# A hand-written queue of 782 entries, put into another order, with 113 of its copies on other engines

## The chip, the core and the metric

The kernel runs on one core of a Trainium2 chip. The metric is the device time of one execution in microseconds (us); of several runs the median counts. The core's engines work at the same time, each through its own queue in order: TensorE (PE; PEld is its weight load), VectorE (DVE), ScalarE (ACT), GpSimd (POOL) and SyncE (SP), which here issues nearly all DMA transfers.

## The reference

Attention with a few global keys and a local window, then a feed-forward layer with three first matrices of which the largest product counts. There are 4 batches, 8 heads, 768 positions and 64 dimensions a head; 8 global keys and a window of 96.

```python
keep = is_global | is_local                    # pos_k < 8, or 0 <= pos_q - pos_k < 96
scores = scale * (q @ k.T) - slope[h] * dist   # dist is capped to 96 at the global keys
a = softmax(where(keep, scores, -1e9))
x = (a @ v) as 3072 tokens of 8 heads * 64
h = maximum(maximum(x @ w1, x @ w2), x @ w3)   # 512 -> 768
out = h @ w_out                                # 768 -> 512
```

## The kernel before, in words

The 3072 tokens are 24 tiles T of 128, six to a batch. A tile attends to itself and to the tile ahead of it. The 8 global keys and their values are copied into the place of keys that are out of the window, in each tile that serves as the one ahead (G for keys, V for values), so that two key tiles are enough; for a batch's first tile G saves the global keys instead. The feed-forward part takes the tiles in seven chunks of 4, 2, 2, 4, 4, 4 and 4.

The whole order is written out by hand in the string SCHEDULE (lines 24 to 87). Each entry is a call of one of the small functions below; the instructions of each engine stand in its queue in the order of the entries. Nothing else plans: an engine waits at the head of its queue until the inputs are there and the buffer or bank that it writes has been read.

An entry is a letter, its arguments, and after @ the slot of the buffer ring or the PSUM bank that it writes. Its last argument, `how`, names the engine of a copy or cast: 0 is ScalarE, 1 VectorE, 2 GpSimd. So `c1.9.2.1` casts k of tile pair 9, both halves of the heads, on VectorE.

- l, w, q: loads of q, k and v (first argument 0, 1, 2), of w1..w3, of w_out (SP). r, rv and staging are their rings. Pair 12 stands for the first four tiles' q and k.
- c, W, Q: casts of these to bf16 (L195, or L201 in two halves on GpSimd). v: the cast of v into the tile `va` (L254).
- x, y: transposes of q and k through TensorE (L270, L276) and the copies out of PSUM (L283, L287); X: the same by one DMA transpose (L292). Both fill `qkT`.
- b, S: the bias and the scores of tile T, half g of the heads (L335, L349); e: the exponential (L356); m: the product with the mask (L365, L367). B and K make the bias and the mask. D are dummy matmuls.
- G, V: the copies of global keys and values (L313, L315; L321 to L325).
- A: scores times values (L391, L394), n: division by the sum (L402, L403) into `xb`; t, u: transposes of that through TensorE (L418, L421); Z: by DMA (L424). Both fill `xT`.
- F c.f.j: the product of chunk c, block f of 128 hidden columns, with matrix j (L433); f: a copy for j = 0 (L447), the maximum for j = 1 (L449) and j = 2 (L452) into `ht`.
- O: the second product of one tile (L457), o: its copy (L471), s: its store (L477). E is the last chunk's end (L479 to L505), whose banks and staging slots are listed in LAST_BANKS and LAST_STAGES.

PSUM has eight banks: F, O, x and t take one, S, b and A two neighbouring ones.

Of the kernel before, what the change touches and what calls it, by code (L numbers as in the profile page):

```python
# [21 lines left out]


SCHEDULE = """
    l0.12.1@0 l1.12.1@1 D10.512@0 l1.12.3@2 l0.12.2@3 l0.12.3@4 R K7 K6 B1.1 K4 B2.1 K2 B3.0 K1 K5 B0.1 B6.1
    K0 c0.12.3.2@0 l1.12.2@5 c0.12.1.1 B4.1 B5.1 c1.12.1.1@1 K3 x12.0.1@0 y0.0.1.0@0 B7.1 l2.0.2@0 D3.256@1
    x12.1.1@1 b0.1@2 v1.0.2 l2.1.2@1 c1.12.3.1 v1.1.2 b1.0@4 y0.1.1.0 b1.1@6 S1.1.1 l0.2.2@6 c0.12.2.1
    y1.0.1.1@1 y1.1.1.0 x12.0.2@0 e1.1@0 c1.12.2.1 x12.0.3 y0.0.0.1 l1.2.2@0 y1.0.0.1 x12.1.3@1 x12.1.2
    y0.1.0.0 S0.1.1 e0.1@1 G0.1 b2.1@6 v2.0.2 v3.0.2 w1.0@0 S1.0.1 G1.0 e1.0@2 b2.0@2 w0.0@0 y1.1.0.1 S2.1.1
    w1.1@1 S0.0.0@0 e0.0@3 l2.2.2@2 S2.0.1 v0.0.1 e2.0@4 w0.1@1 v0.1.1 m0.0.1 e2.1@5 v2.1.2 b3.0@4 A1@0  # L30
    V1.1.1 V1.0.2 G2.1 v3.1.2 w0.2@2 A0@2 S3.0.1 e3.0@6 b3.1@6 n1@0 c0.2.2.2@2 S3.1.1 G3.0 A2@0 V2.0.2
    e3.1@7 V2.1.2 n0@1 t0@2 W0.0.2 c1.2.2.1 u0.0@0 x2.1.2@3 y2.1.2.0@2 w1.2@2 x2.0.2@2 A3@4 t1@6 u1.0 n2@2
    y2.0.2.1 t2@7 n3@3 l0.3.2@1 l1.3.2@2 S4.1.0@0 V3.1.2 e4.1@0 V3.0.2 S4.0.0@2 W1.1.2 u2.1 t3@6 G4.1 u3.0
    W2.0.1 S5.1.0@4 e5.1@2 S5.0.0@0 e5.0@1 m4.1.1 W1.0.1 e4.0@3 F0.5.0@7 F0.4.0@6 W2.1.0 F0.3.0@4 f0.3.0.0@0
    F0.2.0@5 f0.4.0.1@1 F0.1.0@6 v4.1.2 v4.0.2 l2.3.2@0 f0.1.0.0@2 q2@0 v5.1.0 F0.0.0@0 F0.5.1@1 F0.4.1@4
    F0.2.1@6 m4.0.1 f0.0.0.0@3 v5.0.0 f0.5.0.0@4 m5.1.1 A4@2 V4.1.0 F0.3.1@0 W0.1.2 f0.4.1.1 W0.2.0 m5.0.1
    f0.5.1.1 F0.0.1@1 F0.1.1@4 V4.0.1 W1.2.0 n4@1 t4@7 A5@2 W2.2.0 c1.3.2.2@0 f0.0.1.1 f0.1.1.1 F0.1.2@1
    n5@0 u4.1@1 f0.1.2.1@0 F0.0.2@4 q0@1 t5@7 u5.0 q1@2 f0.3.1.1 f0.0.2.1 F0.2.2@2 F0.3.2@3 f0.3.2.1
    c0.3.2.0 f0.2.0.0@2 f0.2.1.1 F1.2.0@4 F1.0.2@7 Q2.0 v7.1.2 F1.0.0@5 f1.0.0.1@3 v6.1.2 F1.0.1@3 f0.2.2.1
    f1.0.1.1 f1.2.0.1@0 Q0.2 f1.0.2.1@1 x3.1.2@6 y3.1.2.1@3 F0.4.2@5 f0.4.2.1 l1.4.2@3 v6.0.2 Q1.2 F1.1.0@0  # L40
    F1.2.2@1 l0.4.2@4 l1.6.2@5 F1.2.1@4 f1.2.1.1 F1.3.1@2 f1.2.2.1 F1.3.2@3 v7.0.2 F1.3.0@4 f1.3.0.0@2
    f1.3.1.1 f1.3.2.1 x3.0.2@1 F0.5.2@5 f0.5.2.1 F1.4.0@2 F1.1.1@3 f1.1.0.0@3 y3.0.2.0 S6.0.0@0 S6.1.0@4
# [17 lines left out]
    l2.9.2@2 l0.8.2@5 c0.8.2.2@0 v19.0.2 V13.0.0 f3.2.0.0@0 v14.0.2 F3.5.1@0 l2.8.2@1 F3.2.1@6 f3.2.1.1  # L60
    f3.2.2.1 F3.3.1@1 F3.5.2@3 v18.1.0 X14@3 v14.1.2 X15 f3.5.1.1 f3.3.1.1 F3.4.1@2 c1.8.2.0 S14.0.0@4
    S14.1.0@0 e14.0@6 G14.2 f3.4.1.1 F3.4.2@6 f3.5.2.1 F3.3.2@7 e14.1@7 f3.4.2.1 m14.0.1 m14.1.1 v19.1.2
    v15.0.2 S15.0.0@0 e15.0@0 S15.1.0@2 G15.1 e15.1@5 f3.3.2.1 O2.0@6 A14@0 V14.1.2 o2.0.1@6 n14@3 X18@0
    O2.1@7 v18.0.0 o2.1.0@7 m15.0.1 S18.0.0@0 S18.1.0@2 X19 Z13@1 V14.0.1 O3.3@6 m15.1.1 e18.0@3 e18.1@4
# [6 lines left out]
    G19.0 s0.1 V19.0.2 s2.1 f4.1.1.1 f4.1.2.1@0 V19.1.1 F4.0.0@4 F4.4.1@5 A17@2 c1.10.2.0 f4.0.0.1@3 n17@2
    F4.5.1@7 f4.5.1.1 F4.2.1@1 F4.3.2@4 f4.5.2.1 f4.4.1.1 F4.0.2@2 F4.3.1@3 F4.4.2@5 f4.2.1.1 v22.1.1
    f4.0.1.1 f4.3.1.1 f4.0.2.1 f4.3.2.1 F4.2.2@1 Z17 F5.1.1@0 F5.2.0@3 F5.5.0@2 s1.1 F5.3.0@4 F5.0.0@6
    f4.2.2.1 f5.3.0.0@4 f5.0.0.0@3 v21.1.2 F5.1.0@1 s0.0 l1.11.2@0 F5.3.1@4 c1.11.2.2 f5.2.0.1@0 f4.4.2.1
    v23.0.2 F5.0.1@3 v21.0.2 f5.1.0.1@2 f5.1.1.1 s2.0 X20@2 S20.0.0@0 v22.0.1 S20.1.0@6 f5.0.1.1 G20.2
    f5.5.0.0@1 e20.0@3 e20.1@4 F5.5.1@2 f5.5.1.1 F5.2.2@3 v20.1.2 f5.3.1.1 F5.2.1@5 m20.1.1 F5.4.0@2
    f5.2.1.1 m20.0.1 f5.2.2.1@1 F5.1.2@4 f5.1.2.1 X21 f5.4.0.0@0 s3.3 X23@3 s0.3 S21.1.0@0 S21.0.0@6 e21.0@2
    F5.0.2@3 X22 f5.0.2.1 v23.1.2 e21.1@6 s0.2 A20@4 F5.4.1@2 V20.0.1 m21.0.1 F5.4.2@3 G21.1 S22.1.0@0
# [533 lines left out]
```

## Time and profile before

| | |
|---|---|
| median of three runs | 175.69 us (175.66 to 176.38) |
| the profiled execution | 176.69 us, span 174.8 us |
| busy: PE, DVE, ACT, POOL | 165.9, 131.9, 95.4, 54.7 us |
| DMA | 37.36 MB, 214 GB/s on average |
| TensorE's granted clock | 0.996 over the span |

The span runs from the first to the last instruction of the program; the execution's own time has 1.9 us around it. Times in the rows are from the span's start. In a group's row stand, behind x and the count, the busy time in us, the mean of one in ns, then the engine's idle time ahead of the group and what ended most of it. A row of the timeline or of the chain gives start and length in us. A row of the windows gives the stretch, its length, then busy us and instructions of each engine, the granted clock of TensorE, the share of the DMA engines and GB/s. In the row of a wait stand the total, the number of times and the longest.

### The profile page before, as it was taken

Reading aid. Unit: us, or ns where it says so; the run is one execution under the profiler, and the core shown is the slowest. Engines: PE = TensorE matmul, PEld = TensorE weight load, DVE = VectorE, ACT = ScalarE, POOL = GpSimd, SP = SyncE. Lnnn points to the kernel's source line nnn. Section 1 sums busy time; section 2 is a strip of 40 time slices with the busy share of each in tenths; the row PEclk is TensorE's granted clock in tenths of the full one; section 3 lists DMA queues with packets and bytes.
Section 4 is the critical chain, followed back from the end, with each engine's and each line's share of the span. In section 5 each row is a group of like instructions: output and inputs, shape, how many; then the busy total and the mean of one; then the engine's idle time right before and its main releaser. Section 6 shows DMA issues by size and latency. Waiting matters only on the chain.

```text
span 174.8 us, 3865 instructions
## 1 busy us (share of the span) xinstructions
PE 165.9 (95%) x1485; PEld 93.6 (54%) x1507; DVE 131.9 (75%) x268; ACT 95.4 (55%) x147; POOL 54.7 (31%) x99
## 2 busy tenths in 40 slices
...
GB/s 149 352 292 327 402 360 385 270 371 311 229 303 179 139 183 266 267 290 284 165 135 112 114 145 306 305 210 260 231 213 20 0 120 137 121 286 4 0 119 185
DMA packets 66403, 37.36 MB, mean 214 GB/s; under 512 B 24144, under 2 KB 61392, under 8 KB 66384
## 3 DMA queue, kind: packets, MB, share of 16 engines
...
q8 instruction: 12, 0.20, 0.5%
...
## 4 chain that ended last, share of the span: by engine, by line
PE 76%; DVE 10%; DMA 6%; ACT 3%; issue 2%; SPq 0%; DVEq 0%
PE psum L433 44%; PE psum L457 17%; PE psum L349 6%; DMA xT<-xb 3%; DMA rawqk<-in_k_dram 3%; DVE P L365 3%; PE psum L391 3%; PE psum L394 2%; PE psum L276 2%; DVE ht L452 1%; DVE xb L403 1%; ACT P L356 1%; PE psum L270 1%; DVE qb L195 1%; PE psum L335 1%
## 5 line engine op out<-in xcount | busy, mean ns | idle before, releaser
L433 PE MATMUL psum<-xT,w 128*128 128x512 bf16 (+1 forms) x491 | 97.5, 348 | 1.5 <-DMA xT<-xb 0.7
L433 PEld LDWEIGHTS <-w 128*128 128x128 bf16 x504 | 47.6, 98 | 42.9 <-DMA xT<-xb 0.9
L356 ACT ACTIVATE P<-psum 128x1024 bf16<-128x1024 f32 (+1 forms) x48 | 43.3, 954 | 10.4 <-PE psum L349 10.3
L449 DVE TENSOR_TENSOR h<-h,psum 128x512 bf16<-128x512 bf16 (+1 forms) x42 | 25.0, 605 | 15.9 <-PE psum L433 12.4
L457 PE MATMUL psum<-wo,ht 128*128 128x512 bf16 (+2 forms) x147 | 33.4, 362 | 0.5
L447 ACT CAST h<-psum 128x512 bf16<-128x512 f32 (+1 forms) x27 | 13.8, 523 | 33.1 <-PE psum L433 29.8
L452 DVE TENSOR_TENSOR ht<-h,psum 128x512 bf16<-128x512 bf16 (+1 forms) x42 | 26.2, 644 | 2.1 <-PE psum L433 0.9
L365 DVE TENSOR_TENSOR P<-P,wmask 128x1024 bf16<-128x1024 bf16 x34 | 25.2, 752 | 2.0 <-ACT P L356 1.7
L457 PEld LDWEIGHTS <-ht 128*128 128x128 bf16 x156 | 13.8, 98 | 13.5 <-DVE ht L452 0.2
L254 POOL CAST va<-rawv 64x512 bf16<-64x512 f32 x28 | 18.5, 668 | 4.8 <-DMA rawv<-in_v_dram 3.7
L323 POOL COPY va<-vaf 4x260 int32<-4x260 int32 x17 | 7.2, 424 | 34.9 <-PE psum L394 34.5
L403 DVE TENSOR_TENSOR xb<-psum,rz 128x512 bf16<-128x512 f32 x24 | 16.6, 692 | 0.8
L201 POOL CAST qb<-rawk 128x512 bf16<-128x512 f32 x12 | 7.5, 654 | 23.7 <-DMA rawk<-in_k_dram 23.7
L349 PE MATMUL psum<-qkT 64*128 64x128 bf16 x352 | 14.4, 217 | 0.5 <-DVE qkT L315 0.4
L391 PEld LDWEIGHTS <-P 128*128 128x128 bf16 x192 | 12.6, 97 | 3.2 <-ACT P L356 0.4
L349 PEld LDWEIGHTS <-qkT 64*128 64x128 bf16 x352 | 10.0, 94 | 7.9 <-issue 5.9
L391 PE MATMUL psum<-va,P 128*128 128x65 bf16 x160 | 12.7, 193 | 0.7 <-DVE ht L452 0.6
L447 DVE CAST h<-psum 128x512 bf16<-128x512 f32 (+1 forms) x15 | 9.1, 615 | 5.1 <-PE psum L433 5.1
L471 ACT COPY staging<-psum 128x512 f32<-128x512 f32 x14 | 8.2, 592 | 8.8 <-PE psum L457 8.8
L201 POOL CAST qb<-rawq 128x512 bf16<-128x512 f32 x14 | 8.9, 664 | 9.0 <-DMA rawq<-in_q_dram 5.0
L394 PEld LDWEIGHTS <-P 128*128 128x128 bf16 x160 | 10.5, 97 | 2.1 <-issue 0.7
L394 PE MATMUL psum<-va,P 128*128 128x65 bf16 x128 | 9.9, 193 | 0.0
...
## 6 DMA issues: line engine op xcount, KB each, us to landing
...
```

The lines of the kernel that those rows point to most:

```text
L254: copies[how](heads(va(T))[64 * e:64 * e + 64, :, 0:D], src)
L349: nc.tensor.matmul(sp[:, hh, j2, ds], qT(T - ds, 1, hsl, jp), qT(T, 0, hsl, jp), start=not how, stop=True, skip_group_check=True)
L356: nc.scalar.activation(P[:, :, 0:n], sps[T, g].rearrange("p a b d n -> p (a b) d n")[:, :, 0:n], AF.Exp, bias=0.0, scale=scale)
L365: mul(P, P, wmask[:, g, :, 0:2])
L391: nc.tensor.matmul(o, P[:, i, 0], heads(va(T))[:, h], start=True, stop=(t == 0), skip_group_check=True)
L394: nc.tensor.matmul(o, P[:, i, 1], heads(va(T - 1))[:, h], start=False, stop=True, skip_group_check=True)
L403: nc.vector.tensor_tensor(out=x.rearrange("p (g h) d -> p g h d", g=2), in0=o4[:, :, :, 0:64], in1=rz[:, :, :, None].to_broadcast([128, 2, ...
L433: nc.tensor.matmul(ps, w123[f // 2][:, j, dm, (f % 2) * 128:(f % 2) * 128 + 128], xT[c][:, dm], start=(dm == 0), stop=(dm == 3))
L447: copies[how](h01, ps)
L449: nc.vector.tensor_max(h01s[c, f], h01s[c, f], ps)
L452: nc.vector.tensor_max(dst, h01s[c, f].rearrange("p (t e i) -> p t e i", e=2, i=64), ps.rearrange("p (t e i) -> p t e i", e=2, i=64))
L457: nc.tensor.matmul(po, ht[c][:, f, tt * 128:(tt + 1) * 128], wo[:, f, cols], start=(f == 0), stop=(f == NF - 1))
```

## The change

Only the string SCHEDULE, LAST_BANKS and LAST_STAGES differ. Both strings have the same 782 entries, if one leaves aside the slots and the engines: every function is called as often and on the same data. The order differs almost everywhere, and 113 entries name another engine. By kind, counted from the entries (ScalarE, VectorE, GpSimd, before and after):

| entry | before | after |
|---|---|---|
| v | 6, 10, 32 | 14, 8, 26 |
| V | 4, 11, 17 | 9, 7, 16 |
| c | 4, 8, 14 | 7, 8, 11 |
| G | 9, 8, 3 | 8, 5, 7 |
| B | 1, 7, 0 | 3, 4, 1 |
| y | 8, 6, 0 | 9, 5, 0 |
| u | 6, 3, 0 | 5, 4, 0 |
| W | 4, 2, 3 | 3, 2, 4 |
| Q | 1, 0, 2 | 0, 0, 3 |
| f | 27, 99, 0 | 26, 100, 0 |
| o | 14, 6, 0 | 13, 7, 0 |

The parts of the diff of which the prediction speaks:

```diff
@@ -22,76 +22,76 @@
 
 
 SCHEDULE = """
-    l0.12.1@0 l1.12.1@1 D10.512@0 l1.12.3@2 l0.12.2@3 l0.12.3@4 R K7 K6 B1.1 K4 B2.1 K2 B3.0 K1 K5 B0.1 B6.1
-    K0 c0.12.3.2@0 l1.12.2@5 c0.12.1.1 B4.1 B5.1 c1.12.1.1@1 K3 x12.0.1@0 y0.0.1.0@0 B7.1 l2.0.2@0 D3.256@1
-    x12.1.1@1 b0.1@2 v1.0.2 l2.1.2@1 c1.12.3.1 v1.1.2 b1.0@4 y0.1.1.0 b1.1@6 S1.1.1 l0.2.2@6 c0.12.2.1
-    y1.0.1.1@1 y1.1.1.0 x12.0.2@0 e1.1@0 c1.12.2.1 x12.0.3 y0.0.0.1 l1.2.2@0 y1.0.0.1 x12.1.3@1 x12.1.2
-    y0.1.0.0 S0.1.1 e0.1@1 G0.1 b2.1@6 v2.0.2 v3.0.2 w1.0@0 S1.0.1 G1.0 e1.0@2 b2.0@2 w0.0@0 y1.1.0.1 S2.1.1
-    w1.1@1 S0.0.0@0 e0.0@3 l2.2.2@2 S2.0.1 v0.0.1 e2.0@4 w0.1@1 v0.1.1 m0.0.1 e2.1@5 v2.1.2 b3.0@4 A1@0
-    V1.1.1 V1.0.2 G2.1 v3.1.2 w0.2@2 A0@2 S3.0.1 e3.0@6 b3.1@6 n1@0 c0.2.2.2@2 S3.1.1 G3.0 A2@0 V2.0.2
-    e3.1@7 V2.1.2 n0@1 t0@2 W0.0.2 c1.2.2.1 u0.0@0 x2.1.2@3 y2.1.2.0@2 w1.2@2 x2.0.2@2 A3@4 t1@6 u1.0 n2@2
...
-    G6.2 c1.4.2.2@1 c0.4.2.2 l0.5.2@0 c0.5.2.2@2 f1.1.1.1 f1.4.0.0@1 e6.0@4 S7.0.0@6 S7.1.0@2 l1.5.2@6
-    c1.5.2.2 e6.1@5 c1.6.2.2@0 e7.1@6 F1.4.1@0 e7.0@7 l2.4.2@1 O0.2@1 f1.4.1.1 m7.1.1 x4.1.2@0 F1.5.2@2
-    F1.5.0@3 m7.0.1 v8.1.2 F1.5.1@4 A7@6 f1.5.0.1@0 m6.1.1 m6.0.1 o0.2.0@0 y4.1.2.0@0 f1.5.1.1 f1.5.2.1
-    x4.0.2@3 y4.0.2.0 G7.0 l0.6.2@1 c0.6.2.2 F1.4.2@5 O0.1@4 f1.4.2.1 n7@2 o0.1.1@1 A6@0 l2.5.2@2 S8.1.0@2
-    S8.0.0@6 n6@3 V7.1.1 G8.1 v8.0.2 F1.1.2@4 O0.3@5 t6@0 v11.0.2 v9.0.2 v9.1.2 f1.1.2.1 V7.0.0 t7@1 e8.1@0
-    e8.0@3 S9.0.0@2 u6.0@2 S9.1.0@6 m8.1.1 u7.1 o0.3.0@2 O0.0@4 e9.1@1 m8.0.1 o0.0.0@3 e9.0@2 F2.4.0@5
...
-    m10.1.1 e11.0@0 f2.0.0.0@1 A10@2 V10.0.2 f2.1.1.1 m11.1.1 o1.0.0@4 n10@3 Z8@0 V10.1.0 l0.7.2@2 v11.1.2
-    v15.1.2 v12.1.2 F2.5.2@0 O1.1@1 v12.0.2 S12.1.0@2 e12.1@3 S13.1.0@4 m11.0.1 Z9 f2.5.2.1 S13.0.0@6
-    o1.1.1@5 F2.4.2@0 A11@2 n11@2 F2.0.1@1 e13.1@1 F2.3.1@4 m12.0.1 m12.1.1 e13.0@2 c0.7.2.1@1 Z10 f2.0.1.1
-    m13.1.1 F2.0.2@5 f2.3.1.1 t11@2 F2.1.2@3 l0.9.2@3 l1.8.2@4 u11.0 G13.0 f2.1.2.1 f2.0.2.1 F2.3.2@6
-    F3.4.0@2 F3.0.0@1 f3.4.0.0@4 f3.0.0.1@0 m13.0.1 v13.1.1 f2.4.2.1 F3.1.0@4 F3.3.0@5 c0.9.2.0@2 f3.3.0.0@1
-    A12@2 n12@1 f2.3.2.1 f3.1.0.1@2 F3.1.1@1 f3.1.1.1 v13.0.1 l1.9.2@0 c1.9.2.1 F3.0.2@0 F3.0.1@5 f3.0.1.1
...
-    X16@1 o3.3.0@8 A15@0 n15@2 O3.0@7 S19.1.0@0 v17.1.1 m18.0.1 S16.1.0@2 m18.1.1 e19.1@1 S16.0.0@4 O3.2@6
-    o3.0.1@9 e16.0@2 V15.1.2 A18@0 e16.1@6 n18@0 o3.2.1@10 m16.1.1 X17 O3.1@7 G16.0 Z14 o3.1.0@11 m16.0.1
-    V15.0.1 S17.0.0@0 v16.0.0 Z12 S19.0.0@2 Z15 e19.0@7 S17.1.0@4 e17.1@0 m17.1.1 F4.4.0@6 e17.0@5 l0.11.2@1
...
-    V16.0.2 m19.0.1 l0.10.2@3 F4.0.1@0 F4.1.1@7 m19.1.1 f4.4.0.0@1 F4.5.2@6 c0.10.2.2@2 A19@2 Z16 n19@1 Z19
...
-    S22.0.0@6 G22.0 e22.1@1 f5.4.1.1 e22.0@7 m21.1.1 f5.4.2.1 V20.1.1 n20@0 O4.0@2 m22.1.1 F5.3.2@3 f5.3.2.1
-    A21@0 n21@3 m22.0.1 S23.1.0@4 e23.1@0 S23.0.0@6 e23.0@5 O4.1@3 F5.5.2@0 m23.1.1 Z21@0 V21.1.1 m23.0.1
-    V21.0.2 A22@4 V22.0.2 V22.1.1 n22@1 s3.2 Z20 o4.1.0@4 O4.3@1 A23@6 O4.2@3 Z22 o4.3.0@11 f5.5.2.1 O5.2@0
-    O5.3@1 n23@2 O5.1@4 o5.3.0@1 Z23 F6.4.2@1 o4.0.1@7 F6.0.0@2 F6.0.2@5 F6.0.1@6 o5.2.0@5 F6.1.2@0 o5.1.0@3
...
+    l0.12.1@0 l1.12.1@1 D10.512@0 l1.12.2@2 l0.12.3@3 l0.12.2@4 R B3.0 B6.2 K7 B1.0 B5.0 K6 K0 B2.1 K1
+    l1.12.3@5 B7.1 c0.12.1.1@0 B4.1 x12.0.1@0 l2.0.2@0 K3 c1.12.1.1@1 y0.0.1.0@0 b0.1@2 c1.12.2.2 c0.12.3.1
+    B0.1 x12.1.1@1 y0.1.1.0 b1.1@4 y1.1.1.1@1 c0.12.2.2 x12.1.2@6 y1.0.1.0 l2.1.2@1 S0.1.1 e0.1@0 v1.0.2
+    S1.1.1 e1.1@1 x12.0.3@7 x12.0.2 l0.2.2@6 c1.12.3.1 y0.0.0.1 b1.0@0 x12.1.3 b2.1@2 y0.1.0.0 D3.256@4
+    S1.0.1 K2 G0.0 l1.2.2@0 y1.0.0.1 e1.0@2 G1.2 y1.1.0.1 b2.0@4 w1.0@0 v1.1.2 S0.0.0@6 w0.0@0 v0.1.1 v3.1.2
+    S2.0.1 S2.1.1 e0.0@3 v0.0.1 b3.1@0 v3.0.2 v2.1.2 e2.1@4 G2.0 A1@6 w1.1@1 v2.0.2 m0.0.1 V1.0.2 e2.0@5
+    A0@2 S3.1.1 e3.1@6 c0.2.2.2@2 n1@0 V1.1.1 b3.0@6 n0@1 S3.0.1 e3.0@7 A2@0 G3.0 V2.0.2 l2.2.2@2 t1@2 t0@3
+    c1.2.2.1 u1.0@0 w0.1@1 x2.1.2@4 y2.1.2.0@2 V2.1.2 x2.0.2@2 n2@2 y2.0.2.1 A3@0 n3@3 t2@5 S4.1.0@6 u2.0
+    S4.0.0@4 e4.1@1 G4.2 t3@2 S5.1.0@0 W1.0.2 u3.0 u0.1 W1.1.2 W2.0.1 W0.0.1 S5.0.0@6 e5.1@2 e5.0@0 e4.0@3
...
+    f1.5.0.1@3 O0.2@3 l2.4.2@1 v8.1.2 e6.0@7 l1.6.2@6 m6.1.1 m7.0.1 x4.1.2@2 y4.1.2.0@0 F1.3.2@4 F1.4.2@5
+    m7.1.1 G6.1 G7.0 m6.0.1 c1.5.2.0 F1.5.1@0 f1.4.2.1 f1.5.1.1 A7@6 V7.1.1 n7@2 f1.3.2.1 x4.0.2@1 y4.0.2.0
+    O0.1@0 l0.6.2@1 o0.2.0@0 A6@6 n6@3 S8.1.0@4 c0.6.2.2@0 V7.0.1 o0.1.0@1 S8.0.0@2 t7@1 F1.1.2@0 G8.1
+    e8.1@1 t6@6 u6.1@2 u7.0 v8.0.2 O0.3@7 e8.0@3 f1.1.2.1 c1.6.2.1 m8.0.1 m8.1.1 o0.3.0@2 F2.5.0@6 l2.5.2@2
...
+    v10.1.1 e10.0@6 V9.1.2 X12@2 o0.0.1@3 G10.2 n9@1 v10.0.1 O1.0@0 F2.2.1@1 f2.2.1.1 o1.0.0@4 m10.1.1 X13
+    V9.0.1 m10.0.1 S11.0.0@2 S11.1.0@4 S12.0.0@6 e12.0@4 F2.1.1@0 F2.2.2@1 f2.2.2.1@0 O1.1@6 e11.0@7 A10@2
+    f2.1.1.1 l2.6.2@0 v12.1.2 e11.1@1 o1.1.0@5 m11.0.1 F2.3.0@7 n10@2 F2.5.2@6 f2.3.0.0@2 V10.1.2 S12.1.0@0
+    S13.1.0@4 e12.1@3 l0.7.2@2 Z8@0 V10.0.2 v12.0.2 G12.2 m11.1.1 l2.7.2@1 Z9 e13.1@0 S13.0.0@2 F2.4.2@7 Z10
+    A11@0 l1.7.2@3 f2.5.2.1 l1.8.2@4 l1.9.2@5 F2.1.2@6 e13.0@2 v13.1.0 F2.0.2@4 n11@3 F2.0.1@5 t11@0 u11.0
+    f2.4.2.1 F2.3.1@1 F2.3.2@7 c1.7.2.0@1 m12.0.1 l0.9.2@0 c0.7.2.2 c0.9.2.2@2 m12.1.1 A12@2 f2.3.1.1
+    v15.1.2 f2.0.1.1 f2.0.2.1 F3.5.2@0 F3.1.0@1 n12@0 v13.0.0 F3.5.0@2 F3.5.1@3 f2.3.2.1 F3.0.0@7 F3.3.0@4
+    m13.0.1 f2.1.2.1 m13.1.1 f3.5.0.1@4 c1.8.2.0@0 f3.5.1.1 F3.4.0@5 f3.4.0.0@1 f3.5.2.1@1 A13@2 F3.1.1@0
+    F3.3.1@5 F3.4.1@6 n13@1 f3.3.0.0@3 f3.3.1.1 f3.1.0.1@2 f3.1.1.1 c1.9.2.0 f3.4.1.1 F3.4.2@4 f3.4.2.1
...
+    O3.3@6 v16.1.2 v18.0.2 S18.1.0@0 V14.1.0 S19.1.0@4 m15.0.1 v17.1.0 m15.1.1 e18.0@3 e18.1@4 A15@2
+    o3.3.0@7 o2.1.1@8 e19.1@0 O3.2@7 o3.2.0@9 S19.0.0@0 G15.2 m18.0.1 v19.0.1 n15@3 m19.1.1 m18.1.1 X16@1
+    S16.0.0@2 S16.1.0@4 G16.1 e19.0@2 e16.1@5 V15.1.1 v19.1.1 O3.1@6 o3.1.0@10 e16.0@6 X17 A18@0 O3.0@7
+    S17.1.0@4 Z13 n18@0 S17.0.0@0 Z14 e17.0@1 m19.0.1 A19@2 n19@1 m17.0.1 Z15 F4.2.1@6 F4.3.0@0 e17.1@7
+    F4.0.2@1 V15.0.0 F4.0.0@2 F4.2.0@3 m16.0.1 m17.1.1 f4.0.0.0@1 m16.1.1 A16@4 V16.0.1 n16@2 f4.2.0.0@0
...
+    S22.0.0@4 G22.1 e22.0@5 X23 F5.4.2@1 O4.1@6 e22.1@6 m21.1.1 f5.4.2.1 S23.1.0@2 S23.0.0@0 o4.1.0@3 Z20@0
+    m22.1.1 m22.0.1 V20.1.2 A21@4 V21.1.2 V21.0.2 n21@2 F5.3.2@6 f5.3.2.1 O4.0@7 e23.0@1 m23.0.1 e23.1@7
+    A22@0 V22.1.2 O5.2@6 V22.0.0 s0.3 m23.1.1 n22@0 s3.2 A23@0 n23@3 Z21 O5.3@2 s3.3 o5.2.1@8 s4.1 O5.1@3
+    O4.2@6 Z22 O4.3@0 o4.2.1@5 s3.1 o5.1.0@11 Z23 F6.3.2@1 F6.2.0@3 F6.3.0@6 f6.3.0.0@1 F6.0.2@4 F6.0.0@5
...
-LAST_BANKS = (6, 7, 3, 0, 1, 4, 5, 2)
-
-LAST_STAGES = (8, 2, 0, 10, 11, 7, 6, 3, 4, 9, 1, 5)
+LAST_BANKS = (5, 4, 6, 7, 1, 2, 0, 3)
+
+LAST_STAGES = (2, 9, 7, 3, 10, 8, 1, 5, 11, 6, 0, 4)
```

65 lines of the change are left out of this document (31 added, 34 removed).

## The prediction

> **What bounds the kernel now.** I read the page's first part, then the windows, the waits of PE, the chain, and last the timelines of single stretches.
>
> ```profile
> PE 165.9 (95%) x1485; PEld 93.6 (54%) x1507; DVE 131.9 (75%) x268; ACT 95.4 (55%) x147; POOL 54.7 (31%) x99
> core 0: us, PE busy (x) PEld busy (x) DVE busy (x) ACT busy (x) POOL busy (x), PEclk, DMA share, GB/s
> 70.00:75.00 5.00, 4.29 (x32) 2.67 (x32) 4.23 (x11) 2.58 (x5) 0.00 (x0) 1.00 1.07 270
> 80.00:85.00 5.00, 4.41 (x35) 2.33 (x35) 4.18 (x7) 1.17 (x3) 3.03 (x5) 1.00 1.13 249
> 110.00:115.00 5.00, 4.83 (x50) 2.73 (x50) 4.29 (x9) 0.62 (x1) 1.03 (x2) 1.00 1.44 284
> 170.00:174.80 4.80, 1.16 (x6) 0.31 (x4) 0.00 (x0) 0.75 (x2) 0.00 (x0) 0.86 0.58 207
> PE psum L433 <- DMA xT<-xb: 0.7, 1, 0.7
> PE psum L391 <- DVE ht L452: 0.6, 1, 0.6
> ```
>
> TensorE is the bound: 165.9 of 174.8 us. Of the 8.9 us in which it stood idle, 3.6 lie in the last window, behind its last matmul. The holes in the middle are few: 0.71 at 70 to 75 (a matmul of L433 waits for the DMA transpose that fills `xT`), 0.59 at 80 to 85 (the matmul of L391 waits for VectorE at L452), 0.17 at 110 to 115. A busy PE may hide waits, so I check its pace in the chain.
>
> ```profile
> 21.58 0.38 PE psum L433
> 22.01 7.50 PE psum L433 x34
> 67.78 4.98 DMA xT<-xb
> 72.81 0.39 PE psum L433
> 131.66 0.55 PE psum L349 x16
> 142.15 1.29 PE psum L457 x6
> 155.42 9.23 PE psum L433 x42
> ```
>
> Early and late the pace is one: 7.50/34 = 0.221 us and 9.23/42 = 0.220 us for each recorded 512-column matmul. With 0.216 us for a matmul (1.29/6) an F entry of a four-tile chunk is 0.86 us, one of a two-tile chunk 0.43, an O entry 1.29, two S entries 0.55. The first F starts at 21.58. So no reordering can speed TensorE's work itself; it can only remove waits, some 1.5 us in the middle, or make new ones.
>
> **The sum starts from** the profiled execution, 176.69 us (span 174.8 and 1.9 around it), 1.0 above the median of 175.69; the difference that I work out is put on both.
>
> **What the change keeps.** Both queues hold the same 782 entries, so PE's matmuls, the exponentials, the masks, the transposes and the transfers are the same in number. SP's list keeps its first two loads and, from l2.0.2 to w1.2, the next eleven in order. What changes is the order elsewhere, the bank or slot of many entries, and the engine of 113 copies, casts and small products. Counted from the entries:
>
> ```profile
> L254 POOL CAST va<-rawv 64x512 bf16<-64x512 f32 x28 | 18.5, 668 | 4.8 <-DMA rawv<-in_v_dram 3.7
> L254 ACT CAST va<-rawv 64x512 bf16<-64x512 f32 x4 | 2.5, 618 | 0.0
> L254 DVE CAST va<-rawv 64x512 bf16<-64x512 f32 x8 | 3.4, 423 | 0.1
> L325 DVE COPY va<-vaf 4x520 bf16<-4x520 bf16 x11 | 4.2, 381 | 0.9 <-PE psum L394 0.8
> L325 ACT COPY va<-vaf 4x520 bf16<-4x520 bf16 x4 | 2.5, 621 | 7.9 <-PE psum L394 7.9
> L201 POOL CAST qb<-rawk 128x512 bf16<-128x512 f32 x12 | 7.5, 654 | 23.7 <-DMA rawk<-in_k_dram 23.7
> L195 ACT CAST qb<-rawk 128x1024 bf16<-128x1024 f32 x2 | 2.1, 1046 | 1.0 <-DMA rawk<-in_k_dram 0.9
> L315 DVE COPY qkT<-kg 128x32 bf16<-128x32 bf16 x6 | 1.6, 275 | 0.0
> ```
>
> ScalarE gets 8 more v entries (8 x 0.618), 5 more V (5 x 0.621) and 3 more c (3 x 1.046): 11.2 us. The small moves (two B and a y gained; a W, a Q, a u, an o, an f and a G lost) take back about 2.4, so ScalarE goes from 95 to about 104 us. VectorE loses two v (0.85), four V (1.52), three G (0.83) and, on balance, small pieces: about 3 us less, 129. GpSimd loses six v (4.0) and three c (six halves of 0.654, 3.9), and gains four G, one W, one Q and a B: about 4 us less. None of this counts by itself, since TensorE is the bound. It counts where one of these queues runs late for a matmul.
>
> **Start, up to the first F.** The new queue puts b0.1 between the two first transposes, moves the dummy matmuls D3.256 behind b2.1, and defers K2, K5 and K4, while ScalarE takes B1 and B5.
>
> ```profile
> 11.32 3.54 ACT L356 ACTIVATE P<-psum 128x1024 bf16<-128x1024 f32 x4
> 15.35 1.02 ACT L356 ACTIVATE P<-psum 128x1024 bf16<-128x1024 f32 x1 [0.49 <-PE psum L349]
> 20.95 0.58 ACT L421 COPY xT<-psum 128x512 bf16<-128x512 bf16 x1
> ```
>
> ScalarE's exponentials set this stage, with one gap of 0.49 in front of the fifth of them. In the new order D3.256 and b1.0 stand ahead of S1.0.1, and K2 and G0.0 ahead of e1.0, so I put the first of the four about 0.13 late; G2 runs on ScalarE inside the row of exponentials (0.2), and the gap of 0.49 closes, because b3.1 and S3.1.1 come before b3.0. Sum: 0.13 + 0.2 - 0.49, about -0.1, and the last link (t3, e4.1, u3.0, F0) is the old one. I take **0**; bounds -0.5 (the gap) and +0.5 (the same size the other way, if G1, now on GpSimd behind v1.0.2, holds up S2).
>
> **From 44 us to the first F3.** c1.5.2 goes to ScalarE, directly ahead of y4.0.2, and o0.2, o0.1 follow that; o0.1 frees bank 0, which F1.1.2 needs.
>
> ```profile
> 50.41 1.01 ACT L287 COPY qkT<-psum 128x1024 bf16<-128x1024 bf16 x1 [0.95 <-PE psum L276]
> 65.45 3.55 SPq L424 DMA_TRANSPOSE xT<-xb  x2
> xT<-xb SPq DMA_TRANSPOSE x15, 3.4
> ```
>
> Before y4.0.2 ScalarE stood idle for 0.95 us, and the cast takes 1.05, so y4.0.2 is hardly later. The two o copies behind it (0.59 each) end near 52.7, about when PE reaches F1.1.2. I take **+0.2**; bounds 0 and +1.0 (the cast itself, if its transfer is late and the idle time doesn't cover it).
>
> Then the gate of F3: Z10, the last transpose of its tokens, was issued at 67.78 and landed 4.98 later, and PE stood still for 0.7. In the new queue A10 has two F2 entries more ahead of it (0.86 us), so n10 and Z10 come 0.4 later, near 68.2, for VectorE had some slack there. With 3.4 to landing (the median row) that is 71.6, with the 4.98 of this one 73.2. PE is ready at 72.8 - 0.75 + 0.26 = 72.3, the 0.26 being A12, which now stands ahead of F3. The old order would have got as far at 72.8 + 0.26 = 73.1. So F3 starts between 72.3 and 73.2; in the middle, 72.7, it has gained 0.35. I take **-0.35**; bounds -0.75 (the wait gone) and +0.5 (0.4 of delay passed on in full).
>
> **F3.** A13 waited for a bank that VectorE emptied late.
>
> ```profile
> 79.97 1.13 DVE L195 CAST qb<-rawk 128x1024 bf16<-128x1024 f32 x1
> 83.12 0.19 PE L391 MATMUL psum<-va,P 128*128 128x65 bf16 x1 [0.59 <-DVE ht L452]
> ```
>
> In the new queue c1.9.2 (the 1.13) is ScalarE's, as are c1.7 and c1.8, and of F3's own stage VectorE's list up to n13 shrinks from eleven entries to three (f3.5.0, f3.5.1, f3.5.2), while A13 stands only four F (3.45 us) earlier, on banks 2 and 3 that f3.5.0 and f3.5.1 free early. The 0.59 goes. What is late next: n13 and f3.3.1 now stand ahead of f3.1.0 and f3.2.0, and I find F3.2.2, S14.1.0 and A14 arriving within 0.2 us of the read that frees their banks. I take -0.6 + 0.2 = **-0.4**; bounds -0.6 and +0.3.
>
> **F4 and the ScalarE queue.** A19 moves from the middle of F4 to ahead of it.
>
> ```profile
> 108.19 2.86 DVE L365 TENSOR_TENSOR P<-P,wmask 128x1024 bf16<-128x1024 bf16 x2
> 108.54 1.16 POOL L201 CAST qb<-rawq 128x512 bf16<-128x512 f32 x2
> 137.83 0.68 DVE L365 TENSOR_TENSOR P<-P,wmask 128x1024 bf16<-128x1024 bf16 x1
> 85.00:105.00 20.00, 19.68 (x196) 10.14 (x198) 16.00 (x32) 14.44 (x20) 3.83 (x8) 1.00 0.77 130
> L356 ACT ACTIVATE P<-psum 128x1024 bf16<-128x1024 f32 (+1 forms) x48 | 43.3, 954 | 10.4 <-PE psum L349 10.3
> L471 ACT COPY staging<-psum 128x512 f32<-128x512 f32 x14 | 8.2, 592 | 8.8 <-PE psum L457 8.8
> ```
>
> The two masks before A19 took 2.86 us beside GpSimd's casts, where one takes 0.68 alone; they cost PE the 0.17 at 110 to 115. In the new queue these casts run elsewhere, and the 0.17 goes. But A19 takes the banks that e16.0 reads, and from e14.0 to e16.0 ScalarE now has eight exponentials (8 x 0.95), two of half the size (1.0), four o (4 x 0.59), c0.8.2 (1.05), a v and a V (1.24) and a G (0.2): 13.5 us. The PE work from S14 to A19 is three F (2.6), six O (7.7), S for six tiles (3.0) and three A (1.3): 14.6. That is nearly full, where the old queue had 14.44 of 20. I take **-0.15**; bounds -0.2 and +1.5 (a rival below).
>
> Of the masks the Trainium skill, "SBUF — State Buffer", section "Who interferes with whom", says that a VectorE instruction with two SBUF inputs and a GpSimd instruction that reads SBUF block each other outright. The 2.86 agrees. By that rule the moved casts give VectorE relief, and the added G, W and Q on GpSimd speak against the change: each can hold up a mask. With GpSimd's total down by 4 of 54.7 the rule's net would be a tenth of a microsecond or two on VectorE, which does not alter the sum.
>
> **F5 and F6.** A23 now uses bank 0 directly after A22, with only O5.2 (1.29) between.
>
> ```profile
> 143.00 0.69 DVE L403 TENSOR_TENSOR xb<-psum,rz 128x512 bf16<-128x512 f32 x1
> L402 DVE RECIPROCAL rz<-psum 128x8 f32<-128x8 f32 x24 | 4.8, 201 | 4.5 <-PE psum L394 2.5 <-PE psum L391 1.0 <-ACT P L356 0.9
> ```
>
> n22 must read it in between: 0.20 + 0.69, some 0.3 of hand-over at both ends, and 0.25 of queue (f5.3.2 and two masks stand ahead): 1.44 against 1.29. I take **+0.15**; bounds 0 and +0.5. Z23 still has four O entries, 5.2 us, over it, so F6 isn't touched; nor is the tail, though LAST_BANKS and LAST_STAGES are permuted.
>
> **Sum:** 0 + 0.2 - 0.35 - 0.4 - 0.15 + 0.15 = -0.55. The profiled execution would take 176.1, the median **175.2 us**. About 0.5% (0.9 us, so 174.8 and 176.6) is what a measurement can tell from no change, and this lies within.
>
> **Rivals.** *The waits go and nothing takes their place.* 0.75 + 0.59 + 0.17 = 1.5 us: **174.2**. For it: VectorE is lighter by 3 us, and all three holes have it or a late transpose at their root. Against: in-order queues of this density have kept PE waiting somewhere in each third of the run. *ScalarE becomes the bound between S14 and A19.* It has 13.5 of 14.6 us; hand-overs and the cast c0.8.2, which waits for a load that stands far back on SP's list, eat the 1.1 that is left. Each microsecond lost beyond that delays e16.0, A19, and with it all of F4. A loss of 2.6 us in all costs 1.5; with the other terms only breaking even, the run takes 175.69 + 1.5, **177.2**. It decides from about 1.1 us of ScalarE idleness in that stretch. For it: the old queue left ScalarE idle there for 5.6 of 20 us. Against: most of that idling was for want of work, and S18 now runs early to feed it. *The transposes still gate F3*, whatever VectorE does: then F3 starts at 73.2 and the sum is -0.1, a part of the forecast.
>
> **Chances.** Forecast 0.42, its own range 174.8 to 176.4. Waits gone 0.32. ScalarE the bound, 0.26. So faster 0.32, same 0.42, slower 0.26. The range takes in both rivals' times, which leaves out about 2 in 10 beyond them: 174.0 to 177.2.
>
> **What would show it.** The window 70 to 75 with PE at 4.5 or more and F3's first matmul near 72.7; no wait of L391 for L452 at 80 to 85; ACT near 104 us and DVE near 129 in the first part; a wait of A23 of at most 0.4 near 141. The forecast is wrong if F0 starts more than 0.5 from 21.6, if the idle time of PE in the middle sums to over 2.5 us, or if A19's matmuls wait for ScalarE at L356.

## The result, and the profile after

The changed kernel takes 177.94 us (median of four runs, 177.80 to 178.01) where the kernel before, run beside it, takes 176.03: a ratio of 1.012, with an interval of 1.0097 to 1.0142. It is slower, and 177.94 lies above the upper end of the forecast range. The profiled execution took 178.01 us with a span of 176.2; the one of before had 176.69 and 174.8. So the pair of traces shows 1.4 us of a difference of 1.9 in the medians; the profiled execution of before was itself 0.66 us above its median.

The changed kernel's first part of the page, its windows, waits of TensorE (PE), and the group of the masks:

```profile
PE 166.2 (94%) x1486; PEld 93.8 (53%) x1507; DVE 131.9 (75%) x258; ACT 104.7 (59%) x160; POOL 51.8 (29%) x95
70.00:75.00 5.00, 4.01 (x62) 3.47 (x55) 4.68 (x9) 3.51 (x5) 1.46 (x4) 1.00 0.63 130
80.00:85.00 5.00, 4.95 (x37) 2.54 (x37) 2.98 (x6) 2.62 (x5) 3.01 (x5) 1.00 0.96 196
110.00:115.00 5.00, 4.95 (x38) 2.52 (x38) 3.16 (x6) 3.77 (x7) 0.00 (x0) 1.00 1.17 298
PE psum L391 <- DVE P L365: 1.0, 1, 1.0
PE psum L457 <- DVE h L449: 0.5, 1, 0.5
L365 DVE TENSOR_TENSOR P<-P,wmask 128x1024 bf16<-128x1024 bf16 x34 | 26.6, 805 | 4.2 <-ACT P L356 4.2
```

TensorE's work is the same (166.2 us, 165.9 before). Of the three holes of before, those at 80 to 85 and at 110 to 115 are filled: 4.95 of 5 us. The wait of F3 for the DMA transpose is gone from the list too. In the window 70 to 75, though, PE fell from 4.29 to 4.01, and behind the first F two waits are new: one of 1.0 us for a mask (L365) and one of 0.5 for a maximum (L449). The mask's group in the kernel before:

```profile
L365 DVE TENSOR_TENSOR P<-P,wmask 128x1024 bf16<-128x1024 bf16 x34 | 25.2, 752 | 2.0 <-ACT P L356 1.7
```

The same 34 masks took 1.4 us more in all. Where that fell is seen in the timelines of the changed kernel (start, length). First 69 to 73 us:

```profile
69.64 2.37 DVE L365 TENSOR_TENSOR P<-P,wmask 128x1024 bf16<-128x1024 bf16 x1
71.93 0.43 DVE L452 TENSOR_TENSOR ht<-h,psum 128x256 bf16<-128x256 bf16 x1
69.59 0.61 POOL L254 CAST vaf<-rawv 64x512 bf16<-64x512 f32 x1
70.15 0.20 POOL L313 COPY kg<-qkT 128x32 bf16<-128x32 bf16 x1
70.30 1.16 POOL L201 CAST qb<-rawq 128x512 bf16<-128x512 f32 x2
72.07 0.20 PE L391 MATMUL psum<-va,P 128*128 128x65 bf16 x1 [0.99 <-DVE P L365]
```

One mask, m11.1, took 2.37 us. It lasted through four instructions of GpSimd in a row: the cast v12.0, the copy G12 and both halves of the cast c0.7.2. G12 and c0.7.2 are two of the 113 entries that changed engine, from VectorE to GpSimd. The mask ended at 72.01, 0.55 after the last of them (71.46), and A11's matmuls stood still for 0.99 us. Then 24 to 31 us and 47 to 53 us:

```profile
24.47 3.96 DVE L365 TENSOR_TENSOR P<-P,wmask 128x1024 bf16<-128x1024 bf16 x4 [2.00 <-ACT P L356]
27.02 0.76 PEld L433 LDWEIGHTS <-w 128*128 128x128 bf16 x5 [0.44 <-ACT w L195]
29.73 0.10 PEld L391 LDWEIGHTS <-P 128*128 128x128 bf16 x1
48.25 1.95 DVE L365 TENSOR_TENSOR P<-P,wmask 128x1024 bf16<-128x1024 bf16 x2 [0.22 <-ACT P L356]
48.03 1.63 POOL L201 CAST qb<-rawq 128x512 bf16<-128x512 f32 x2 [2.26 <-DVE P L367]
50.12 0.58 DVE L313 COPY kg<-qkT 128x32 bf16<-128x32 bf16 x1
51.28 0.41 DVE L449 TENSOR_TENSOR h<-h,psum 128x256 bf16<-128x256 bf16 x1
52.89 0.44 DVE L452 TENSOR_TENSOR ht<-h,psum 128x256 bf16<-128x256 bf16 x1
50.92 1.04 ACT L195 CAST qb<-rawk 128x1024 bf16<-128x1024 f32 x1
51.87 1.00 ACT L287 COPY qkT<-psum 128x1024 bf16<-128x1024 bf16 x1
51.74 1.46 PE L457 MATMUL psum<-wo,ht 128*128 128x512 bf16 x5 [0.54 <-DVE h L449]
53.03 0.42 PE L391 MATMUL psum<-vaf,P 128*128 128x65 bf16 x8
53.48 0.62 PE L349 MATMUL psum<-qkT 64*128 64x128 bf16 x16
```

and the same places in the kernel before:

```profile
24.33 1.71 DVE L365 TENSOR_TENSOR P<-P,wmask 128x1024 bf16<-128x1024 bf16 x2
29.14 0.10 PEld L391 LDWEIGHTS <-P 128*128 128x128 bf16 x1
47.19 0.69 DVE L365 TENSOR_TENSOR P<-P,wmask 128x1024 bf16<-128x1024 bf16 x1 [0.26 <-ACT P L356]
48.10 0.69 DVE L365 TENSOR_TENSOR P<-P,wmask 128x1024 bf16<-128x1024 bf16 x1 [0.23 <-ACT P L356]
52.11 0.42 PE L391 MATMUL psum<-vaf,P 128*128 128x65 bf16 x8
52.46 0.62 PE L349 MATMUL psum<-qkT 64*128 64x128 bf16 x16
```

At 27 us F0.4.1 waits 0.44 for its weights: their cast W2.1 now stands behind K5, K4 and V3.1 on ScalarE. Four masks in a row took 3.96 us there, and the weight loads of A4, the first A entry behind F0's first products, start 0.59 later than before (29.73, 29.14). At 51.7 the second product O0.1 waits 0.54 for the maximum f1.5.1, which frees its bank and which stands on VectorE behind two masks of together 1.95 us (0.69 each before) and G6 of 0.58. The first S8 loses only 0.1: it starts 0.45 behind A6 (53.48 and 53.03), before 0.35 (52.46 and 52.11). What ended last ahead of it is the maximum f1.3.2 on VectorE (52.89 and 0.44 long), which reads the bank that S8.1 writes and stands behind the division n7. The copy y4.0 (51.87), which stands behind the cast c1.5.2 (50.92), moved to ScalarE, had ended 0.46 before that.

### The profile page after: what moved, and what is told of

It is laid out like the page before. It is cut to its first block, busy times and chain, and to the rows that moved or that the text cites. A ratio compares the mean times of both kernels' runs of the same rounds, so it can differ in the third digit from the quotient of the medians.

```text
span 176.2 us, 3870 instructions
## 1 busy us (share of the span) xinstructions
PE 166.2 (94%) x1486; PEld 93.8 (53%) x1507; DVE 131.9 (75%) x258; ACT 104.7 (59%) x160; POOL 51.8 (29%) x95
## 4 chain that ended last, share of the span: by engine, by line
PE 66%; DMA 15%; DVE 9%; SPq 3%; issue 2%; ACT 2%; POOL 2%; DVEq 0%; POOLq 0%
PE psum L433 40%; PE psum L457 16%; DMA staging<-in_moe_w_dram 6%; DMA rawv<-in_v_dram 6%; PE psum L349 5%; DMA rawqk<-in_k_dram 3%; DVE P L365 3%; PE psum L391 2%; PE psum L394 2%; DVE h L449 2%; SPq L514 1%; SPq L229 1%; DVE ht L452 1%; POOL w L201 1%; DVE h L447 1%
## 5 line engine op out<-in xcount | busy, mean ns | idle before, releaser
L356 ACT ACTIVATE P<-psum 128x1024 bf16<-128x1024 f32 (+1 forms) x48 | 43.6, 957 | 13.6 <-PE psum L349 13.4
L447 ACT CAST h<-psum 128x512 bf16<-128x512 f32 (+1 forms) x26 | 13.2, 525 | 36.1 <-PE psum L433 28.7
L365 DVE TENSOR_TENSOR P<-P,wmask 128x1024 bf16<-128x1024 bf16 x34 | 26.6, 805 | 4.2 <-ACT P L356 4.2
L449 DVE TENSOR_TENSOR h<-h,psum 128x512 bf16<-128x512 bf16 (+1 forms) x42 | 25.0, 605 | 6.2 <-PE psum L433 3.5
L452 DVE TENSOR_TENSOR ht<-h,psum 128x512 bf16<-128x512 bf16 (+1 forms) x42 | 26.4, 642 | 2.0 <-PE psum L433 0.8
L254 POOL CAST va<-rawv 64x512 bf16<-64x512 f32 x20 | 13.9, 699 | 2.8 <-DMA rawv<-in_v_dram 2.1
L402 DVE RECIPROCAL rz<-psum 128x8 f32<-128x8 f32 x24 | 4.9, 203 | 8.5 <-PE psum L394 7.5
L471 ACT COPY staging<-psum 128x512 f32<-128x512 f32 x13 | 7.6, 591 | 5.3 <-PE psum L457 5.1
```

The lines of the kernel that those rows point to most:

```text
L254: copies[how](heads(va(T))[64 * e:64 * e + 64, :, 0:D], src)
L356: nc.scalar.activation(P[:, :, 0:n], sps[T, g].rearrange("p a b d n -> p (a b) d n")[:, :, 0:n], AF.Exp, bias=0.0, scale=scale)
L365: mul(P, P, wmask[:, g, :, 0:2])
L447: copies[how](h01, ps)
L449: nc.vector.tensor_max(h01s[c, f], h01s[c, f], ps)
L452: nc.vector.tensor_max(dst, h01s[c, f].rearrange("p (t e i) -> p t e i", e=2, i=64), ps.rearrange("p (t e i) -> p t e i", e=2, i=64))
```

## The experiments

All are edits of the string SCHEDULE. The ratio is to the kernel before, run on the same chip; the changed kernel has 1.012. The explanation under test is that **entries newly on GpSimd hold up masks on VectorE**, and that TensorE waits for those. Its rivals are the **order** of the queues by itself, and the **row of transfers**: that they land one behind the other at a pace of their own and take back what compute gains.

**Engines apart from order (x1, x2).** x1 has the new order with the old engines, x2 the reverse.

> The order, banks and slots of the changed kernel, with all 113 entries put back on the engine that the kernel before names. If the engines are the cause (masks on VectorE that stand beside the casts and copies newly given to GpSimd): 176.9 us or less, the mask of tile 11 near 0.7 us where it took 2.37, F2.1.2 without its wait of 1.2 us. If the order and the reuse of banks are the cause: 177.5 us or more, with the waits at A6 and at the first S8 (0.9 us together) still there; the mixture can also bring new waits, since this order was made for other engines, and then it is above 178.5.

> The order, banks and slots of the kernel before, with the 113 entries on the engines of the changed kernel. If the engines are the cause: at least 1 us over the kernel before, 177.0 us or more, with masks of 1 us and over beside GpSimd's casts. If the order is the cause: within 0.6 us of the kernel before. Above 179 the mixture itself has made a new wait, and the run tells little.

Measured: 195.61 us (ratio 1.1096, 1.1046 to 1.1145) and 191.55 (1.0884, 1.0839 to 1.0928). Both mixtures brought waits of their own that are some eight to nine times what is asked, so they say nothing of the cause. They do say that order and engines fit each other in each kernel, and that neither can be carried over without the other.

**The mask at 70 us (x3, x7).** x3 puts two entries back on VectorE, behind f2.5.2 and m12.1; x7 puts them on ScalarE and leaves VectorE's queue as it is.

```diff
-... v12.0.2 G12.2 m11.1.1 ... f2.5.2.1 ... c0.7.2.2 c0.9.2.2@2 m12.1.1
+x3: ... v12.0.2 m11.1.1 ... f2.5.2.1 G12.1 ... c0.9.2.2@2 m12.1.1 c0.7.2.1
+x7: ... v12.0.2 G12.0 m11.1.1 ... f2.5.2.1 ... c0.7.2.0 c0.9.2.2@2 m12.1.1
```

> The changed kernel with two entries back on VectorE and behind the maximum that sets bank 6 free: G12 right after f2.5.2, c0.7.2 right after the mask m12.1. If GpSimd's reads hold up the mask m11.1: that mask falls from 2.37 us to under 1.0, F2.1.2 starts without its wait of 1.2 us, and the time falls by 0.7 to 1.2 us, to about 176.9. If the mask is slow for another reason (its own queue, the exponential of tile 11): it still takes over 1.8 us and the time stays within 0.3 us of 177.9. If the wait goes and Z10 gates F3 again, the time falls by less than 0.4 us.

> The changed kernel with G12 and c0.7.2 on ScalarE, at the same places of the order: VectorE's queue is as in the changed kernel, instruction by instruction, and only two things are gone from beside the mask m11.1, GpSimd's copy and cast. If GpSimd's reads hold VectorE's mask up: m11.1 falls from 2.37 us to 1.4 or less (two casts of values still stand beside it), and F2.1.2 starts at least 0.8 us earlier. If x3 was faster because VectorE's queue was in another order: m11.1 stays over 2 us. The total is about 177.2 by the first, unless ScalarE's cast of 1.05 us delays the exponential of tile 13.

Measured: x3 177.27 (1.0070, 1.0042 to 1.0098), x7 177.39 (1.0072, 1.0042 to 1.0102). The timeline of x7:

```profile
69.71 1.11 DVE L365 TENSOR_TENSOR P<-P,wmask 128x1024 bf16<-128x1024 bf16 x1
69.66 0.61 POOL L254 CAST vaf<-rawv 64x512 bf16<-64x512 f32 x1
```

With only GpSimd's copy and cast gone and VectorE's queue untouched, the mask fell from 2.37 to 1.11 us. It still outlasts the one cast that stays beside it (until 70.27) by 0.55 us, as it had outlasted the last of four. F2.1.2, which stands behind A11, came 1.10 us earlier (times of entries are of their first weight load), in x3 1.39. So the hold-up by GpSimd is shown. What my expectation for x3 had put down to bank 6 and f2.5.2 is A11's own wait for the mask, as the row of 72.07 says.

Here the Trainium skill, "SBUF — State Buffer", section "Who interferes with whom", agrees: by it a VectorE instruction with two SBUF inputs and a GpSimd instruction that reads SBUF exclude each other for whole instructions. The 0.55 us left to the mask after the last read, nearly the 0.68 of a mask alone, is what such a lock looks like. That the two slow each other in proportion, sharing a bandwidth, would not give it.

**The queue at 24 to 30 us (x5).**

```diff
-K5 ... K4 ... V3.1.0 W2.1.0 ... f0.3.0.1@0 ... V3.0.0 ... f0.4.0.0@1 ... f0.4.1.1 f0.5.0.0@2 ... f0.0.0.0@3 f0.1.0.1@4
+K5 ... K4 ... W2.1.0 ... f0.4.0.0@1 f0.3.0.0@0 V3.1.0 V3.0.0 ... f0.1.0.1@4 f0.4.1.1 f0.0.0.0@3 f0.5.0.0@2
```

> The changed kernel with the queue between 24 and 30 us mended: on ScalarE the cast W2.1 and the copy f0.4 go ahead of the copies V3, the copy f0.3 goes from VectorE to ScalarE, and f0.1 on VectorE goes ahead of the maximum f0.4.1. If the order there costs what the trace shows (0.55 us more than before between the first F0 and F0.0.1): F0.4.1 starts by 26.7 (27.02) and A4 by 29.3 (29.73), and the time falls by 0.4 to 0.6 us from 177.9, if nothing later takes it back. If transfers pace what follows (the loads of pairs 3 to 5 and the transposes): the gain of 0.5 at 30 us is under 0.2 us at 45 us, and the time stays.

Measured: 177.82 us (1.0093, 1.0063 to 1.0123). A4 starts at 29.20, 0.53 earlier, as expected; at 33 us 0.28 of it is left. At 72 us the run is 0.51 ahead (F2.1.2 at 71.78), for O0.1 waits only 0.30 in it, and it stays so to the end of F4. But F5 starts at 120.59 where it had started at 120.61: what was won is handed back there. F5 had waited for nothing in the changed kernel; here it waits 0.6 for the DMA transpose Z17.

**The queue at 51 us (x4, x6, x12).** x4 and x6 were built on the reading that A6 waited 0.54 us for the division n7 and the first S8 0.37 for y4.0. The rows above bear out neither: it is O0.1 that waits, for f1.5.1, and S8 comes behind f1.3.2.

```diff
-... c1.5.2.0 ... A7@6 V7.1.1 n7@2 ... y4.0.2.0 ... n6@3 ... o0.1.0@1
+x4: ... A7@6 n7@2 ... y4.0.2.0 c1.5.2.0 ... n6@3 V7.1.1 ...
+x6: ... A7@6 n7@2 ... y4.0.2.0 ... n6@3 V7.1.1 ... o0.1.0@1 c1.5.2.0
-m7.1.1 G6.1 G7.0 m6.0.1 c1.5.2.0 F1.5.1@0 f1.4.2.1 f1.5.1.1
+x12: m7.1.1 c1.5.2.2 F1.5.1@0 f1.5.1.1 m6.0.1 f1.4.2.1 G6.1 G7.0
```

> The changed kernel with two moves in the queue near 51 us, engines unchanged: V7.1 goes behind the division n6, so that n7 frees its banks earlier, and the cast c1.5.2 on ScalarE goes behind the copy y4.0.2, on which S8 waits. If the order near 51 us costs what the trace shows (0.54 us ahead of A6 and 0.37 us ahead of the first S8): both waits fall to under 0.2 us each and the time falls by 0.5 to 0.9 us, to about 177.2. If a later wait only grows by what is saved (F2.1.2 and its mask at 70 us): the waits near 51 us go, the one at 70 us grows from 1.2 to about 2 us, and the time stays within 0.3 us of 177.9.

> As x4, but the cast c1.5.2 goes behind the copies o0.2 and o0.1 as well, since in x4 the second S8 waited 0.7 us for o0.2, which stood behind that cast. If the order near 51 us is what costs: A6, both S8 and t7 start without a wait, t7 by 53.4 (54.03), and the time falls by 0.5 to 0.7 us. If it is only handed on: t7 earlier, but F2.1.2 at 70 us at the same time as in the changed kernel (72.3), and the time within 0.3 us of 177.9.

> The changed kernel with the maximum f1.5.1 directly behind the mask m7.1 on VectorE (m6.0, f1.4.2 and G6 follow it; G7 on ScalarE follows G6) and the cast c1.5.2 on GpSimd as in the kernel before. If O0.1 waits for bank 0, which f1.5.1 reads, and the first S8 for y4.0 behind the cast: O0.1 takes 1.3 us instead of 1.71, A6 starts at 52.4 or earlier (52.82), S8.1 within 0.1 us of A6's end, and F2.5.0 by 55.3 (56.01). The time by the compute alone: 177.1 to 177.4. If the row of transfers holds F5 at 120 (Z17 has its place unchanged): it starts no earlier than 119.9, and the time is 177.3 to 177.8. If n7 was the cause after all: A6 stays at 52.6 or later.

Measured: 178.28 (1.0129, 1.0094 to 1.0163), 178.44 (1.0136, 1.0102 to 1.0170) and 178.24 (1.0113, 1.0089 to 1.0136). None gains, and x12 ends above both times that its expectation gave. x4 and x6 moved the wrong thing: in both O0.1 still waited for f1.5.1 (0.2 and 0.4 us), and the cast in its new places held up o0.2 or the exponential of tile 8. x12 did free O0.1, and then the division n7 was the next one late, by about what was won: O0.1 starts 0.66 earlier, A6 0.64 later. Its timeline:

```profile
50.74 0.74 DVE L367 TENSOR_TENSOR P<-P,wmask 128x512 bf16<-128x512 bf16 x1
52.01 0.64 DVE L325 COPY va<-vaf 4x520 bf16<-4x520 bf16 x1
51.27 1.24 POOL L201 CAST qb<-rawk 128x512 bf16<-128x512 f32 x2
51.08 1.46 PE L457 MATMUL psum<-wo,ht 128*128 128x512 bf16 x6
53.67 0.42 PE L391 MATMUL psum<-vaf,P 128*128 128x65 bf16 x8 [1.14 <-DVE xb L403]
```

O0.1 runs without a wait, and A6 now stands 1.14 us for n7. Ahead of n7 the mask m6.0 and the copy V7.1 take 0.74 and 0.64 beside GpSimd's casts, 0.41 and 0.29 in the changed kernel; the cast c1.5.2, which this edit gives back to GpSimd, is one of these. So two entries of VectorE's queue are late at this place, and each edit only changed which of them TensorE met.

**The row of transfers (x9, x10).** In x3 0.65 us of the gain were lost at F5. The chain of x3, and its timeline of PE's weight loads:

```profile
115.18 4.92 DMA xT<-xb
120.20 0.78 PEld L433 LDWEIGHTS <-w 128*128 128x128 bf16 x5 [0.77 <-DMA xT<-xb]
```

Z17 was issued 0.83 us earlier than in the changed kernel (115.18 against 116.01) and landed at the same time, 120.1 (119.99). x9 moves four stores behind it, x10 is x9 and x3 together.

```diff
-... s2.1 V19.1.2 s1.1 Z16 ... s3.0 s0.1 ... Z18 Z17 ... X20 ...
+... V19.1.2 Z16 ... Z18 Z17 ... X20 s2.1 s1.1 s3.0 s0.1 ...
```

> The changed kernel with four stores of the output (s2.1, s1.1, s3.0, s0.1) moved on SyncE's queue from ahead of Z16, Z18 and Z17 to behind X20; nothing else. If the transfers land one behind the other and pace F5 (each store took 0.6 to 0.8 us of the row of landings): Z17 lands at 117.5 to 118.3 where it landed at 119.99. In this kernel F5's first matmul came right behind F4's last (120.61 after 120.49), so the time falls by at most 0.2 us, to 177.7 or 177.9. If Z17 lands at 119.5 or later, its landing isn't a matter of what stands ahead of it.

> x3 and x9 together. In x3 1.17 us were won at F2.1.2, 0.33 given back at F3 and 0.65 at F5, where it waited for Z17. If the row of transfers took those 0.65 back: they stay here, F5 starts by 119.7 and the time is 0.5 to 0.8 us below x3's, 176.5 to 176.8. If something else holds F5 (the copies of chunk 4, the divisions of tile 17): F5 starts after 120.0 again, and the time is that of x3, 177.3.

Measured: x9 177.75 (1.0107, 1.0084 to 1.0131), x10 177.07 (1.0074, 1.0048 to 1.0100). The rows of the transposes' landing, first of the changed kernel's Z17, then of x10's:

```profile
DMA to landing us min/median/max: 4.0/4.0/4.0
DMA to landing us min/median/max: 2.4/2.4/2.4
```

Z17 lands at 118.34 in x9 and 117.25 in x10, and F5 starts in x10 at 119.43 without a wait. So what stands ahead on SyncE's list had set that landing: shown in the trace. That the total follows isn't: the profiled execution of x10 is 0.6 us faster than that of x3, but the ratios (1.0074, 1.0070) are alike.

The runs give a second look at 51 us. Up to 69 us x10's queue is that of the changed kernel, but its cast c0.5.2 happened to start 0.66 earlier. Its timeline:

```profile
47.37 1.36 POOL L201 CAST qb<-rawq 128x512 bf16<-128x512 f32 x2 [2.52 <-DMA rawq<-in_q_dram]
50.20 0.16 DVE L313 COPY kg<-qkT 128x32 bf16<-128x32 bf16 x1
51.41 1.46 PE L457 MATMUL psum<-wo,ht 128*128 128x512 bf16 x6
```

GpSimd was done with v8.1 by 49.75, G6 took 0.16 instead of 0.58, and O0.1 had no wait. So most of that wait, too, comes from VectorE and GpSimd standing beside each other: in the nine profiled runs with this order up to f1.5.1 in which G6 takes 0.58 or 0.59, O0.1 waits 0.30 to 0.62; in the two in which it takes 0.16, it waits 0.21 (x4) and not at all (x10).

**All together (x8, x11, x13, x14, x15, x16).** x8 is x3, x5 and x6; x11 is x8 with x9's stores and, in place of x6, c1.5.2 on GpSimd and V7 behind u6; x13 is x5, x12, x7 and x9; x14 is x13 without x7's edit; x15 is x13 with VectorE's queue at 51 us as below, where the first line is the changed kernel's; x16 is the changed kernel again.

```diff
-m7.1.1 G6.1 G7.0 m6.0.1 c1.5.2.0 F1.5.1@0 f1.4.2.1 f1.5.1.1 A7@6 V7.1.1 n7@2 f1.3.2.1 ... V7.0.1 ... u6.1@2
+x15: m7.1.1 G6.0 G7.0 c1.5.2.2 F1.5.1@0 f1.5.1.1 m6.0.1 A7@6 n7@2 f1.4.2.1 f1.3.2.1 ... u6.1@2 V7.1.1 V7.0.1
```

> The changed kernel with the three edits together: the order at 24 to 30 us (x5), the order at 51 us (x6), G12 and c0.7.2 off GpSimd at 70 us (x3). If compute alone sets the time: the gains add, 0.5, 0.6 and 1.2 us, and it ends near 175.7. If the transfers pace it in part: in x3 Z17 was issued 0.83 us earlier than in the changed kernel and still landed at 120.1 (119.99), and F5 waited for it; then Z17 lands near 120 here as well, Z10 gates F3 at 73.2, and the time is 176.8 to 177.3 whatever was saved ahead.

> The three edits of x8, with the stretch at 51 us mended in another way (the cast c1.5.2 back on GpSimd at its place, V7.1 and V7.0 behind the copy u6 that F2 waits for), and the four stores behind X20. If waits on compute and the row of transfers share the loss: F2.5.0 starts at 55.4 or earlier (56.01), F2.1.2 at 70.3 (72.29), Z10 gates F3 at about 73.5, F5 starts by 119.6, and the time is 176.0 to 176.5, level with the kernel before. If the loads that stand ahead of Z10 and Z12 to Z15 pace the kernel from 60 us on: what is won ahead of 70 us is lost at F3 or at F4, and the time is that of x10.

> x5, x12, x7 and x9 together: the order at 24 to 30 us, f1.5.1 first and c1.5.2 on GpSimd at 51 us, G12 and c0.7.2 on ScalarE at 70 us, four stores behind X20. If the three waits behind VectorE and the row of transfers are the whole loss: gains of 0.25, 0.6 and 1.1 us stay, F5 starts by 119.0 (120.61), and the time is 175.5 to 176.2, level with the kernel before or under it. If there is a further bound between 73 and 100 us (Z10, loads of pairs 7 to 9, Z12 to Z15 landing later than before): F5 not before 119.5, and the time is 176.5 to 176.9, as in x11.

> x13 with one thing put back as in the changed kernel: G12 and c0.7.2 on GpSimd beside the mask m11.1. If the hold-up of that mask has a price of its own: m11.1 takes 2.37 us again, F2.1.2 waits for 1.2 us, and the time is 0.7 to 1.2 us over x13's. If what is won ahead of 70 us moves the mask away from GpSimd's cast, which waits for a load that lands at a fixed time (70.2): m11.1 takes under 1.5 us and the time is within 0.4 us of x13's.

> x13 with the queue at 51 us put in another order: G6 on ScalarE, then on VectorE f1.5.1, m6.0, n7, f1.4.2, f1.3.2, and V7 behind the copy u6. If the queue on VectorE there was the rest: A6 ends by 52.6, the first S8 starts by 52.9 (53.53 in x13, 53.45 in the changed kernel), F2.5.0 by 55.5, and the time is 176.1 to 176.6, 0.6 to 1.0 us under x13, level with the kernel before. If something between 55 and 120 us takes it back (Z10 lands at 73.1, Z15 at 102): F5 starts no earlier than in x13 (119.75) and the time stays at 177.0.

> The changed kernel as it is, on the chip of x15. Both theories expect 177.7 to 178.1 us, the mask m11.1 at 2.37 us, the wait at F2.1.2 and the landing of Z17 near 120. Should the mask or the landing differ, what was read as a price of the order would be chance of one execution.

| | median us | ratio to before, interval |
|---|---|---|
| x8 | 177.53 | 1.0076 (1.0047 to 1.0106) |
| x11 | 176.83 | 1.0056 (1.0035 to 1.0078) |
| x13 | 177.15 | 1.0055 (1.0036 to 1.0075) |
| x14 | 178.13 | 1.0109 (1.0088 to 1.0130) |
| x15 | 176.77 | 1.0030 (1.0011 to 1.0049) |
| x16 | 178.02 | 1.0106 (1.0077 to 1.0134) |

x13 and x14 ran on one chip and differ in two entries' engine: 0.98 us in the medians (x14's runs lie at 178.00 to 178.42, x13's at 176.61 to 178.06). x14's timeline has the mask back at its old length:

```profile
69.95 2.37 DVE L365 TENSOR_TENSOR P<-P,wmask 128x1024 bf16<-128x1024 bf16 x1
```

In x8 the three edits brought 0.4 us in the medians, 0.8 by the ratios; the gains don't add. F5 doesn't wait in it. What A4 had won is gone at O0.1, which stands 0.62 for f1.5.1, and by the order of x6 F2.5.0 starts at 56.57, in the changed kernel at 56.01. x8 and x13 end above both times that their expectations gave, x11 and x15 between the two. x16 repeats the changed kernel: the mask at 2.37, the wait of O0.1 at 0.39, Z17 3.9 us to landing. x15, on one chip with x16, is 1.25 us faster than the changed kernel, with the first S8 at 52.89 (53.45), F2.1.2 at 70.56 (72.29) and F5 at 119.03 (120.61). No version beats the kernel before: x15 is 0.3% above it. Its profiled execution is level with that of before (176.53 and 176.69), so the traces show no place for the last 0.5 us; that stays open.

## Why the prediction was wrong, step by step

- **Start.** Forecast 0; F0 starts at 21.73 by the trace, 21.58 before. Right.
- **24 to 31 us.** No term of the sum covers it: I went from the first F to 44 us, taking F0's own stage as unchanged, though K5, K4 and the copies f0.3 and f0.1 had moved there. Beyond the 0.15 of the start it cost 0.44 us at A4; x5 gave 0.53 back there. The step failed by omission.
- **From 44 us.** Forecast +0.2, on the idle 0.95 us ahead of y4.0.2, with 1.0 as a bound. Measured: 0.54 at O0.1 and 0.1 at the first S8, both behind VectorE, where I had looked at ScalarE's cast and copies and not at VectorE's masks. The cast on ScalarE is not what S8 waited for. The term was mis-sized by 0.4 and put on the wrong engine.
- **The gate of F3.** Forecast -0.35 and F3 at 72.7. The wait for Z10 did go, as in the rival where it goes wholly (0.75), but not as the step had it. Z10 was issued at 69.7, where 68.2 was forecast, and landed at 73.1, later than before (72.8). TensorE came later still: F3 started at 75.05, since A6 was 0.92 late already and A11 had stood 0.99 us for a mask of 2.37. In x7, without most of that hold-up, Z10 lands at 73.7 and F3 starts at 73.86, right behind it. So it is luck that this wait is gone. I had looked there at the transfer alone.

```profile
DMA to landing us min/median/max: 3.4/3.4/3.4
75.05 0.99 PEld L433 LDWEIGHTS <-w 128*128 128x128 bf16 x6
```

- **F3 and F4.** Forecast -0.4 and -0.15. The waits for L452 and at 110 to 115 are gone: 4.95 of 5 us in both windows. Right, and the rival by which ScalarE becomes the bound did not come, though ScalarE went to 104.7 us (104 forecast): no wait of TensorE for L356 there.
- **F5 and F6.** Forecast +0.15; A23 waits for nothing. Nearly right.
- **The lock.** The step that decided. I saw the 2.86 us of two masks beside casts in the trace of before, and took the effect of the change by totals: GpSimd lighter by 4 us, so "a tenth of a microsecond or two". (It got 2.9 lighter.) In that trace one of the two masks took 2.06 by itself, through three casts, and ended 0.55 after the last (109.70): the case of 70 us, at a place where TensorE lost 0.17.

```profile
108.19 2.06 DVE L365 TENSOR_TENSOR P<-P,wmask 128x1024 bf16<-128x1024 bf16 x1
107.98 0.61 POOL L254 CAST va<-rawv 64x512 bf16<-64x512 f32 x1 [0.18 <-DMA rawv<-in_v_dram]
108.54 1.16 POOL L201 CAST qb<-rawq 128x512 bf16<-128x512 f32 x2
```

In the changed kernel the masks got 1.4 us slower in total, not faster; and at one place, where four reads of GpSimd's queue met one mask that TensorE was about to need, the price was 1 us (x14 against x13). VectorE stayed at 131.9 us where 129 was forecast; 1.4 of the 2.9 us are the masks'.

By the trace the terms are +0.15, +0.44, +0.64, +1.0 for the losses, -0.75, -0.6 and -0.2 for the waits that went: +0.7 of the 1.4 us in span. The rest is in small steps that I have not followed. (From 175.69 the sum of -0.55 gives 175.1, not 175.2; that changes nothing.)
